# A written-out instruction order in place of a list scheduler: forward and backward of a strided convolution with group norm and GELU

## The chip, the cores and the metric

The kernel runs on one core of a Trainium2 chip. The metric is the device time of one execution in microseconds (us); smaller is better. A core has five engines that run side by side, each in its own program order: TensorE (PE: matmuls, with the weight loads shown as PEld), VectorE (DVE), ScalarE (ACT), GpSimdE (POOL) and SyncE (SP, which here only issues DMAs). SBUF holds the operands, PSUM (eight banks) the matmul sums. Engines wait for each other by semaphores.

## The reference

`x` is (2, 16000, 256), `w` (31, 256, 256), all in bfloat16. The forward part is a convolution over time with stride 2 and 31 taps, a normalisation of every channel over all 7985 output positions, scale and shift, and a tanh-GELU:

```python
    L = (T - K) // s + 1                     # s = 2, L = 7985
    h = sum over i of einsum('blc,cd->bld', x[:, i:i + s*L:s, :], w[i])
    mu, var = mean and variance of h over l
    h = (h - mu) / jnp.sqrt(var + 1e-5)
    h = h * gn_gamma + gn_beta
    return _gelu(h)
```

The outputs are this forward result and, for a given `grad_out`, the gradients with respect to `x` (out_1), `w` (out_2), `gn_gamma` and `gn_beta`. So there are three convolutions' worth of matmuls: forward, input gradient, weight gradient.

## The kernel before

**Stages.** F0 is the forward convolution of batch 0, F1 that of batch 1 with the GELU work of batch 0 beside it, G0 the input gradient of batch 0 with the GELU work of batch 1 beside it, G1 the input gradient of batch 1, and W the weight gradient in nine combinations n = 0 to 8. Each batch is cut into four chunks c = 0 to 3. The convolutions are split in three (leaves A, B, C, sums of operands made on DVE) so that fewer multiplications are needed; the price is the elementwise work on DVE and ACT that makes the sums and puts the results together.

**PE and PSUM.** The PSUM banks form a ring of four tiles of two banks. In G0 and G1 a tile goes through `g_seed` (earlier results are put in: line L836 on ACT, L1392 on ACT, L1396 on DVE), `g_leaf`, `g_three_b` and `g_three_ac` (the matmuls, L1329; after those of `g_three_b` a copy L1356 on ACT), and `g_evac` (the result to SBUF: `keep`, L836 on ACT, or an addition L1428 on DVE). After the last g_evac of a chunk pair a DMA of 1 MB stores a part of out_1 (`load`, L547, on SP's queue); the buffer it reads is written again by a later g_evac. In F0 and F1 the matmuls are L741, with copies L777 and sums L821, L825 and evacuation L856. In W they are L1564, with copies L1666 and sums L1674 into PSUM; L1630 and L1634 (`pair_x`), L1645 and L1650 (`pair_d`) and L1730, L1735 (`leaf_d`) make the operands on DVE.

**GELU work.** For each of eight units of a batch: two scalings and squares (L1101, L1103 on ACT), a combination (L1106 on DVE), two sigmoids (L1108, L1110 on ACT), a scaling (L1112 on DVE), five products (L1116 on DVE), then sums (L1127 on ACT, L1129 on DVE) and DMA transposes (`turn`, L552, on SP). `e_load` and `e_comp` bring a chunk's gradient from DRAM (tiles hd and dyd) and scale it (L1211 and L1213 on DVE, or L1218 and L1220 on ACT), add it (L1222) and spread it (L1231).

**Queues.** The large loads, stores and transposes are all issued by SP, one after the other; POOL's queue has the stores of the staged gradient (`dl`). Names in DRAM: hd the staged h, dyd and yd the staged gradient and result, dld the sums of the gradient, vl sums of weights, zt zeros.

**What sets the order.** Every operation is first recorded with `add` (engine, estimated time, the operations that must come before it by 32-byte cells of memory: `preds`). `emit` then issues the 3224 operations in the order that `order()` gives and pins it, so that every engine has exactly this order. In the kernel before, `order()` works out a due time for every operation, going back from PE's work, with shifts by kind (`lead`) and by kind and part (`fine`), and `listing` (a list scheduler with its own estimates of engines and DMAs) takes, at each step, the operation that is ready and due first.

Of the kernel before, what the change touches and what calls it, by code (L numbers as in the profile page):

```python
# [37 lines left out]

class Plan:
# [3 lines left out]
    def __init__(self, tc):  # L43
# [7 lines left out]
        self.look = 13  # L51
        self.pads = (3122.5, 3149.5, 2842.0)
        self.lead = {
            "F0 f_evac last": -17.5,
            "F0 f_mm f_leaf": -492.5,
            "F0 f_mm f_outer": -63.0,
            "F0 f_mm f_three_ac": 6.0,
            "F0 f_mm f_three_b": 10.5,
            "F0 f_mm pe_turn": -521.5,
            "F0 f_outer forward": -60.0,  # L60
            "F0 f_seed forward": -47.0,
            "F0 load put": 16.0,
            "F0 tt f_sums": -81.5,
            "F0 tt second": 39.5,
            "F0 tt third": 10.5,
            "F0 turn x_load": -31.0,
            "F0 ve f_seed": -184.0,
            "F0 ve_neg f_seed": 62.5,
            "F0 w_sum w2_part": 38.5,
            "F0 zero x_load": 202.0,  # L70
            "F1 f_evac last": -66.5,
            "F1 f_mm f_leaf": -359.5,
            "F1 f_mm f_outer": -0.5,
            "F1 f_mm f_three_ac": -9.0,
            "F1 f_mm f_three_b": -13.0,
            "F1 f_three_b forward": -29.0,
            "F1 keep f_evac": -8.5,
            "F1 load f_evac": -6.5,
            "F1 load gelu_unit": 7.5,
            "F1 load out0_store": 27.5,  # L80
            "F1 tiny elem_finalize": -18.0,
            "F1 tiny fwd_stats": 17.0,
            "F1 tt f_sums": -78.5,
            "F1 tt gelu_unit": -45.5,
            "F1 tt second": -72.0,
            "F1 tt third": -68.5,
            "F1 turn gelu_batch": 30.0,
            "F1 turn gelu_unit": -36.0,
            "F1 turn x_load": 44.5,
            "F1 ve f_seed": -25.5,  # L90
            "F1 w_sub f_again": 60.0,
            "G0 cp e_comp": -84.0,
            "G0 e_comp e_load": -1.0,
            "G0 g_evac last": -12.5,
            "G0 g_mm g_leaf": -8.5,
            "G0 g_mm g_three_b": -8.0,
            "G0 g_three_b input_grad": 0.5,
            "G0 gelu_batch conv_stem_kernel": -47.0,
            "G0 gelu_unit gelu_batch": -2.0,
            "G0 keep g_evac": -35.5,  # L100
            "G0 keep g_seed": -114.0,
            "G0 load dl_turn": 8.5,
            "G0 load e_load": 38.5,
            "G0 load g_evac": 17.0,
            "G0 load gelu_unit": 2.0,
            "G0 load load_w2": -0.5,
            "G0 spread e_comp": -1.0,
            "G0 tiny elem_finalize": -9.5,
            "G0 tiny fwd_stats": 6.5,
            "G0 tt first": -94.5,  # L110
            "G0 tt gelu_unit": -0.5,
            "G0 tt third": 5.5,
            "G0 turn dgb_store": 6.0,
            "G0 turn dl_turn": 5.0,
            "G0 turn gelu_batch": 7.0,
            "G0 w_sum load_w2": -5.5,
            "G0 zero e_comp": 10.0,
            "G1 cp e_comp": -166.0,
            "G1 e_comp e_load": 13.0,
            "G1 g_evac last": -8.0,  # L120
            "G1 g_mm g_leaf": -160.0,
            "G1 g_mm g_outer": -5.5,
            "G1 g_mm g_three_ac": -9.0,
            "G1 g_mm g_three_b": -33.0,
            "G1 g_three_b input_grad": -10.0,
            "G1 keep g_evac": 3.5,
            "G1 load dl_turn": 11.0,
            "G1 load e_load": -7.5,
            "G1 load g_evac": 9.0,
            "G1 plus g_seed": 1.5,  # L130
            "G1 spread e_comp": -6.0,
            "G1 spread g_seed": -69.0,
            "G1 tt first": -16.5,
            "G1 tt second": -15.0,
            "G1 tt third": -48.5,
            "G1 turn dl_turn": 3.5,
            "G1 w_sum w2_outer": 28.0,
            "G1 zero e_comp": -8.5,
            "W keep w_keep": -78.0,
            "W keep weight_grad": 6.0,  # L140
            "W leaf_d weight_grad": -3.5,
            "W load d_tile": -38.0,
            "W load out0_late": 111.0,
            "W load w_emit": 25.0,
            "W load weight_grad": 52.0,
            "W load x_raw": 1.5,
            "W pair_d weight_grad": -8.0,
            "W pair_x weight_grad": 0.5,
            "W turn out0_late": -42.5,
            "W ve weight_grad": -22.0,  # L150
            "W w_add weight_grad": 1.0,
            "W w_add x_tile": -2.0,
            "W w_both weight_grad": 10.0,
            "W w_emit w_done": -11.0,
            "W w_emit weight_grad": -353.5,
            "W w_mm w_leaf": -12.0,
            "W w_pairs weight_grad": -377.5,
        }
        self.spare = {k + " dl_turn": 3.0 for k in ("G0 turn", "G0 load", "G1 turn", "G1 load")}
        self.room, self.mixed = 2048.0, 2.2  # L160
        self.overlap = {"DVE": 0.084, "ACT": 0.1}
        self.fine = {
            "F0 f_evac last": {0: 23.0, 1: 16.0, 3: 6.5},
            "F0 f_mm f_outer": {0: 131.5, 2: -265.5},
            "F0 f_mm f_three_ac": {0: -57.0, 1: -59.0, 2: -100.5, 3: -14.5},
            "F0 f_mm f_three_b": {1: 8.5, 2: 3.0, 3: -307.0},
            "F0 f_outer forward": {0: 78.5, 3: -25.0},
            "F0 f_three_b forward": {0: 23.0, 3: -69.5},
            "F0 load put": {1: 187.0, 3: 31.5},
            "F0 tt f_sums": {0: -63.0, 2: 5.5},  # L170
            "F0 tt second": {0: 23.5, 1: -168.0, 2: -53.0},
            "F0 tt third": {1: -19.0, 2: -173.5, 3: -0.5},
            "F0 turn x_load": {0: 40.0, 1: 293.5, 2: 52.5, 3: 36.5},
            "F0 ve_neg f_seed": {0: 260.5, 3: 1.0},
            "F0 w_sub f_first": {0: 43.0},
            "F0 w_sum w2_part": {0: 20.0, 1: -74.5, 2: -56.0, 3: 42.0},
            "F0 zero x_load": {3: 7.0},
            "F1 f_evac last": {2: 13.5, 3: 12.0},
            "F1 f_mm f_outer": {3: -48.0},
            "F1 f_mm f_three_ac": {2: 20.0, 3: -4.0},  # L180
            "F1 f_mm f_three_b": {0: 3.0, 1: 48.0, 2: -3.0, 3: -35.0},
            "F1 f_three_b forward": {2: 29.5},
            "F1 gelu_unit gelu_batch": {0: -154.0, 2: -6.5, 3: -13.5, 4: 15.5, 5: -28.5, 6: 24.0, 7: -47.0},
            "F1 keep f_evac": {2: 6.5},
            "F1 load f_evac": {3: 3.5},
            "F1 load gelu_unit": {6: 11.0, 7: -15.5},
            "F1 load out0_store": {0: 7.0, 1: -8.0},
            "F1 tiny elem_finalize": {0: 6.0},
            "F1 tiny fwd_stats": {0: -42.0},
            "F1 tt f_sums": {0: 75.5, 1: -6.5, 2: 24.5},  # L190
            "F1 tt gelu_unit": {5: -38.0},
            "F1 tt second": {1: -25.5},
            "F1 turn gelu_batch": {0: -263.5, 1: -10.5, 3: 96.0},
            "F1 turn gelu_unit": {0: 0.5, 1: 30.5, 2: -17.5, 5: 40.5},
            "F1 turn x_load": {1: 40.5, 2: 9.5, 3: 27.5},
            "F1 ve f_seed": {1: 23.5, 2: 5.0},
            "F1 w_sub f_again": {3: -1.5},
            "G0 e_comp e_load": {0: -10.0, 1: -18.0, 2: -6.0, 3: -6.0},
            "G0 g_evac last": {1: 9.0, 2: 1.5},
            "G0 g_mm g_leaf": {0: -2.5, 2: -7.5},  # L200
            "G0 g_mm g_three_ac": {1: -1.0, 3: 19.0},
            "G0 g_mm g_three_b": {0: -3.0, 1: -5.0, 2: 1.5, 3: -22.0},
            "G0 g_three_b input_grad": {1: 5.0, 2: 14.0, 3: 6.0},
            "G0 gelu_batch conv_stem_kernel": {6: 40.0},
            "G0 gelu_unit gelu_batch": {0: -2.5, 1: -11.0, 3: 2.5, 4: -6.5, 5: -8.5, 6: -7.5},
            "G0 keep g_seed": {0: 122.0},
            "G0 load dl_turn": {0: -29.0, 1: 1.5, 2: -1.5},
            "G0 load e_load": {1: -41.0, 3: -1.0},
            "G0 load g_evac": {1: -16.0, 2: -6.0, 3: 10.5},
# [104 lines left out]
    def order(self):  # L314
# [3 lines left out]
        for i, o in enumerate(ops):  # L318
            for p in o["preds"]:
                succ[p].append(i)  # L320
# [1576 lines left out]
```

## Time and profile before

| what | value |
|---|---|
| time, median of 3 runs (lowest to highest) | 1166.46 us (1164.47 to 1167.01) |
| span of the profiled execution, first to last instruction | 1161.2 us |
| median less span (start and end around it) | 5.3 us |
| PE busy | 1128.5 us, 97% |
| DVE busy | 982.8 us, 85% |
| ACT busy | 554.0 us, 48% |
| POOL busy | 131.7 us, 11% |
| mean granted PE clock | 0.997 |
| moved by DMA | 243.57 MB, mean 210 GB/s |

The profile is one execution. Of the times, no row has the profiled execution's own total beside its span; the median of the runs stands in for it. A timeline row has the start, the busy time, the engine and the line, the operation with output and input, the count of equal instructions in a row, and in brackets the idle time before and what ended it. Successive rows of one engine can overlap by about 0.1 us. A matmul row's line is that of the helper, so tiles and times tell the stages apart: F0 and F1 are up to about 415 us, G0 and G1 to about 842 us, W to the end.

### The profile page before, as it was taken

The page shows a single profiled execution, that of the slowest core. Times are in us where ns is not written, and L with a number is a line of the kernel's source. Part 1 is how long each engine was busy: PE and PEld are TensorE (multiplying, and loading weights), DVE is VectorE, ACT ScalarE, POOL GpSimd, SP SyncE. Part 2 cuts the span into 40 slices and gives each one's busy share as a digit, 9 for nine tenths or more (in the row PEclk, how much of TensorE's full clock was granted, in tenths as well). Part 3 has the DMA queues.
Part 4 walks back from the last instruction along what each step waited for, and adds up shares of the span by engine and source line. Part 5 has one row for each costly group of instructions (what it writes and reads, how often), then busy time and mean ns, then how long its engine had stood idle before and what let it go on. Part 6 is the DMA issues. An engine that isn't in the chain of part 4 may idle for free.

```text
span 1161.2 us, 18913 instructions
## 1 busy us (share of the span) xinstructions
PE 1128.5 (97%) x7700; PEld 753.2 (65%) x7700; DVE 982.8 (85%) x892; ACT 554.0 (48%) x833; POOL 131.7 (11%) x221
## 2 busy tenths in 40 slices
PE   5999999999999999999899999999999999999998
PEld 3888899877777864444344444444488766656685
DVE  7996787699989988998786868768799998699986
ACT  1254454688786588788563545653422212211200
POOL 0000000000000011333232132241200000000000
PEclk9999999999999999999999999999999999999999
DMA  9476738869796699999996886686999726899673
GB/s 217 63 184 127 179 109 164 208 140 200 182 248 141 221 366 255 261 263 231 256 228 192 179 191 163 159 200 175 212 353 289 256 82 221 287 323 320 219 222 104
DMA packets 345807, 243.57 MB, mean 210 GB/s; under 512 B 233377, under 2 KB 316967, under 8 KB 341543
## 3 DMA queue, kind: packets, MB, share of 16 engines
q1 hardware_dynamic: 338615, 223.47, 73.5%
q0 software_dynamic: 7104, 18.89, 6.1%
q8 instruction: 60, 0.98, 0.4%
q14 instruction: 28, 0.23, 0.1%
HBM read 106.24 MB, written 80.25 MB: 161 GB/s over the span
## 4 chain that ended last, share of the span: by engine, by line
PE 80%; DVE 6%; DMA 6%; ACT 3%; SPq 3%; issue 2%; DVEq 0%; ACTq 0%
PE ps L741 33%; PE ps L1329 24%; PE ps L1564 22%; DMA arena<-dld 2%; SPq L547 2%; DMA out_dram<-arena 1%; DMA arena<-hd 1%; SPq L552 1%; DVE arena L1428 1%; ACT arena L836 1%; DMA arena<-dyd 1%; DVE arena L1116 1%; DVE arena L1282 1%; DVE arena L687 1%; DMA arena<-in_x_dram 1%
## 5 line engine op out<-in xcount | busy, mean ns | idle before, releaser
L1329 PE MATMUL ps<-arena 128*128 128x512 bf16 (+1 forms) x1920 | 414.0, 377 | 9.8 <-DVE arena L1428 3.2
L741 PE MATMUL ps<-arena 128*128 128x256 bf16 (+4 forms) x3460 | 406.8, 281 | 14.7 <-DMA arena<-in_x_dram 6.0
L741 PEld LDWEIGHTS <-arena 128*128 128x128 bf16 x3460 | 338.1, 99 | 83.2 <-DVE arena L683 6.4
L1329 PEld LDWEIGHTS <-arena 128*128 128x128 bf16 x1920 | 188.3, 98 | 233.6 <-issue 16.9
L1564 PE MATMUL ps<-arena 128*128 128x256 bf16 (+1 forms) x2320 | 309.2, 296 | 4.1 <-DMA arena<-dld 2.3
L1564 PEld LDWEIGHTS <-arena 128*128 128x128 bf16 x2320 | 226.8, 98 | 86.8 <-DMA arena<-dld 2.1
L836 ACT ACTIVATE arena<-ps 128x1024 f32<-128x1024 f32 (+1 forms) x111 | 113.1, 1022 | 248.9 <-PE ps L1564 86.1
L699 DVE TENSOR_TENSOR arena<-arena 128x2080 bf16<-128x2080 bf16 (+8 forms) x126 | 157.1, 1266 | 27.1 <-PE ps L741 26.4
L547 POOL DMA_DIRECT2D dld<-arena x144 | 104.6, 728 | 295.1 <-DMA arena<-arena 247.8
L1116 DVE TENSOR_TENSOR arena<-arena 128x2048 bf16<-128x2048 bf16 (+1 forms) x80 | 95.6, 1196 | 11.9 <-ACT arena L1110 5.8
L1282 DVE TENSOR_TENSOR arena<-arena 128x1032 bf16<-128x1032 bf16 (+1 forms) x120 | 84.5, 727 | 12.7 <-PE ps L1329 6.6
L1532 DVE TENSOR_TENSOR arena<-arena 128x4096 bf16<-128x4096 bf16 x38 | 86.1, 2285 | 7.9 <-DMA arena<-in_x_dram 5.5
L1396 DVE TENSOR_TENSOR ps<-ps,arena 128x2048 f32<-128x2048 f32 x24 | 55.1, 2298 | 22.3 <-PE ps L1329 21.4
L856 ACT ACTIVATE arena<-ps 128x512 bf16<-128x512 f32 (+1 forms) x64 | 37.0, 580 | 57.9 <-PE ps L741 53.7
L556 POOL MEMSET arena<- 128x128 bf16 (+11 forms) x40 | 8.6, 246 | 403.6 <-ACT ps L777 149.3
L1666 ACT COPY ps<-ps 128x256 f32<-128x256 f32 x54 | 19.3, 358 | 73.2 <-PE ps L1564 72.1
L1396 DVE TENSOR_TENSOR arena<-ps,arena 128x2048 f32<-128x2048 f32 x16 | 36.6, 2290 | 18.7 <-ACT arena L836 15.3
L1356 ACT COPY ps<-ps 128x512 f32<-128x512 f32 x48 | 27.5, 577 | 44.5 <-PE ps L1329 38.6
L1106 DVE SCALAR_TENSOR_TENSOR arena<-arena 128x2048 bf16<-128x2048 bf16 (+1 forms) x16 | 35.8, 2238 | 12.1 <-ACT arena L1103 12.1
L1428 DVE TENSOR_TENSOR arena<-ps,arena 128x1024 bf16<-128x1024 f32 x32 | 38.8, 1219 | 7.7 <-DMA out_dram<-arena 4.6
L1735 DVE TENSOR_TENSOR arena<-arena 128x4608 bf16<-128x4608 bf16 x16 | 40.5, 2552 | 5.7 <-PE ps L1564 5.6
L777 ACT ACTIVATE ps<-ps 128x256 f32<-128x256 f32 x75 | 27.8, 371 | 36.4 <-PE ps L741 35.1
(83 smaller groups left out, 780.4 us busy)
## 6 DMA issues: line engine op xcount, KB each, us to landing
arena<-in_x_dram SPq DMA_DIRECT2D x40, 1024.0 KB
dld<-arena POOLq DMA_DIRECT2D x144, 128.0 KB, 3.8
arena<-hd SPq DMA_DIRECT2D x32, 512.0 KB
out_dram<-arena SPq DMA_DIRECT2D x14, 1024.0 KB
arena<-dld SPq DMA_DIRECT2D x18, 640.0 KB
arena<-dld SPq DMA_DIRECT2D x18, 576.0 KB
vl<-arena SPq DMA_DIRECT2D x36, 256.0 KB
arena<-vl SPq DMA_DIRECT2D x9, 1024.0 KB
```

Of the source, the lines that this page charges most:

```text
L547: lambda: e.dma_start(out=out, in_=in_), dma=np_ * ns / 16e3 * 1.03, ns=ns, tp=SH[pk], slack=slack)
L699: lambda: nc.vector.tensor_tensor(out=o, in0=a, in1=b, op=ALU.add))
L741: yield nc.tensor.matmul(ps[:, dh, cs], lhsT=wt, rhs=mv, start=s0, stop=False, skip_group_check=True)
L836: lambda: nc.scalar.activation(out=out, in_=ps, func=ACT.Copy, scale=scale))
L1116: add("DVE", dve(nf), [o], [a, b_], lambda: V.tensor_tensor(out=o, in0=a, in1=b_, op=op))
L1282: lambda: nc.vector.tensor_tensor(out=o, in0=a, in1=b, op=ALU.subtract))
L1329: yield nc.tensor.matmul(ps[:, e, 0:wide], lhsT=lt, rhs=mv, start=s0, stop=False, skip_group_check=True)
L1396: lambda: nc.vector.tensor_tensor(out=o, in0=a, in1=b, op=ALU.add))
L1428: lambda: nc.vector.tensor_tensor(out=ho[:, :, k, :], in0=ps[:], in1=g, op=ALU.add))
L1532: add("DVE", dve(4096), [o], [a, b], lambda: nc.vector.tensor_tensor(out=o, in0=a, in1=b, op=ALU.add))
L1564: yield nc.tensor.matmul(ps[:, s, c0:c1], lhsT=lt, rhs=mv, start=s0, stop=False, skip_group_check=True)
L1735: add("DVE", dve(4608), [o], [u, v], lambda: nc.vector.tensor_tensor(out=o, in0=u, in1=v, op=ALU.subtract))
```

## The change

`order()` no longer computes anything. The order is a string of 3224 numbers, `SEQUENCE`; `order()` splits it, checks that it holds every operation once and that each comes after its `preds`, and returns it. The due times, the tables of shifts and `listing` are removed. The string stands for an order that was set by moving single instructions. The recorded operations, their operands and their count are the same. Every line after the edit is 237 lower (L836 is L599, L1428 is L1191, L1116 is L879, L1356 is L1119, L547 is L310, L552 is L315, L1218 and L1220 are L981 and L983, L1396 is L1159, L1231 is L994).

Of the operations, those that stand at another place on their engine are: PE 662 of 884 (an operation of PE is a group of matmuls), DVE 776 of 860, ACT 540 of 696, POOL 190 of 217, SP 520 of 567. The mean shift is 2.0 places on PE, 4.5 on DVE, 2.9 on ACT, 3.2 on POOL and 9.3 on SP.

```diff
+SEQUENCE = """
+6 12 5 4 13 3 7 15 9 1 11 22 14 8 2 16 17 31 37 41 32 34 38 40 33 35 23 42 39 36 44 52 25 43 53 50 46 45 47 49 26 48 51 55 24 56 61 54 66 27 67 29 62
...
+"""
...
-        self.fine = {
-            "F0 f_evac last": {0: 23.0, 1: 16.0, 3: 6.5},
...
     def order(self):
-        ops = self.ops
-        n = len(ops)
-        succ = [[] for _ in range(n)]
...
-            due[i] = end - full - self.lead.get(o["kind"], 0.0) - self.fine.get(o["kind"], {}).get(o["part"], 0.0)
-        self.listing(due, succ)
-        return sorted(range(n), key=lambda i: (self.start[i], i))
-
-    def listing(self, due, succ):
...
-                pick = min((i for i in w if ready[i] <= t + 1e-9), key=lambda i: (due[i], i))
...
-        self.start, self.ends = start, ends
+        seq = [int(i) for i in SEQUENCE.split()]
+        assert sorted(seq) == list(range(len(self.ops)))
+        seen = set()
+        for i in seq:
+            assert self.ops[i]["preds"] <= seen
+            seen.add(i)
+        return seq
```

Three places of the order follow.

The first is SP in G0, chunk 2, about 536 to 548 us of the profile before. The rows are DMA issues: a transpose of staged data (L552, L315 after), loads of dyd and hd for `e_load`, a store of the staged gradient dyd_2, the transpose of grad_out, the store of out_1 (out_dram<-arena) and a load of h for the GELU work (hd_3). Before:

```order
L552 DMA_TRANSPOSE arena<-arena 128x4x128 x4
L547 DMA arena<-dyd_0_72 128x2048
L547 DMA arena<-hd_0_64 128x2048
L547 DMA dyd_2_74<-arena 256x1x1024
L552 DMA_TRANSPOSE arena<-in_grad_out_dram 128x8x256
L547 DMA out_dram<-arena 128x4096
L547 DMA arena<-hd_3_67 128x2x1024
```

After:

```order
L315 DMA_TRANSPOSE arena<-arena 128x4x128 x4
L310 DMA dyd_2_74<-arena 256x1x1024
L310 DMA out_dram<-arena 128x4096
L310 DMA dld_8_88<-zt_117 2x256
L315 DMA_TRANSPOSE arena<-arena 128x4x128
L315 DMA_TRANSPOSE arena<-in_grad_out_dram 128x8x256
L310 DMA arena<-hd_3_67 128x2x1024
```

The store of out_1 stood behind the loads of dyd and hd and behind the transpose of grad_out; now it stands ahead of that transpose, and the two loads are elsewhere.

The second is ACT in G1, about 684 to 701 us, where `e_load` for chunk 1 of batch 1 comes up. The rows are copies out of PSUM (`keep`, L836, L599 after), the copies L1356 (L1119 after), and the scalings of hd (L1218, L981 after) and of dyd (L1220, L983 after). Before:

```order
L836 ACTIVATE arena<-ps 128x2x512
L1218 ACTIVATE arena<-arena,stats 128x1024 x2
L836 ACTIVATE arena<-ps 128x1024 x2
L1356 COPY ps<-ps 128x512 x2
L1220 ACTIVATE arena<-arena,stats 128x1024 x2
L836 ACTIVATE arena<-ps 128x2x512 x2
L1356 COPY ps<-ps 128x512
```

After:

```order
L599 ACTIVATE arena<-ps 128x1024
L1119 COPY ps<-ps 128x512
L599 ACTIVATE arena<-ps 128x1024
L1119 COPY ps<-ps 128x512
L981 ACTIVATE arena<-arena,stats 128x1024
L994 COPY arena<-arena 128x256
L599 ACTIVATE arena<-ps 128x2x512 x2
L1119 COPY ps<-ps 128x512
L599 ACTIVATE arena<-ps 128x2x512
L1155 COPY arena<-ps 128x2048
L599 ACTIVATE arena<-ps 128x2x512
L983 ACTIVATE arena<-arena,stats 128x1024
```

The scaling of dyd stood ahead of three `keep`s; now these stand ahead of it.

The third is DVE early in G0, about 438 to 452 us. The rows are g_evacs (L1428, L1191 after), GELU work (L1106, L1112, L1116; L869, L875, L879 after), sums for the next leaves (L1045 after) and the scaling of hd (L974 after, L1211 before). Before:

```order
L1428 TENSOR_TENSOR arena<-ps,arena 128x2x512
L1106 SCALAR_TENSOR_TENSOR arena<-arena 128x2048
L1112 TENSOR_SCALAR arena<-arena 128x2048
L1428 TENSOR_TENSOR arena<-ps,arena 128x2x512
L1116 TENSOR_TENSOR arena<-arena 128x2048
L1428 TENSOR_TENSOR arena<-ps,arena 128x2x512
L1116 TENSOR_TENSOR arena<-arena 128x2048
```

After:

```order
L869 SCALAR_TENSOR_TENSOR arena<-arena 128x2048
L1191 TENSOR_TENSOR arena<-ps,arena 128x2x512
L875 TENSOR_SCALAR arena<-arena 128x2048
L879 TENSOR_TENSOR arena<-arena 128x2048
L1045 TENSOR_TENSOR arena<-arena 128x1032
L1191 TENSOR_TENSOR arena<-ps,arena 128x2x512
L879 TENSOR_TENSOR arena<-arena 128x2048 x2
L974 TENSOR_SCALAR arena<-arena,stats 128x2048
L879 TENSOR_TENSOR arena<-arena 128x2048 x2
L1191 TENSOR_TENSOR arena<-ps,arena 128x2x512
```

Between the second and the third g_evac there was one product; now there are four products and a scaling.

More of the change, by code (lines that the diff above doesn't have):

```diff
@@ L50, in __init__ @@
         self.hold = -1
[L51 to L158, printed above, removed]
```

223 lines of the change are left out of this document (removed), and 100 rows, old and new, of the table SEQUENCE.

## The prediction

> **What bounds the kernel now.** I read the page first, then the list of waits of PE, then windows around each wait, then the timelines of the engines that PE waited for. The page's first rows (busy us, share of the span, instructions):
>
> ```profile
> span 1161.2 us, 18913 instructions
> PE 1128.5 (97%) x7700; PEld 753.2 (65%) x7700; DVE 982.8 (85%) x892; ACT 554.0 (48%) x833; POOL 131.7 (11%) x221
> ```
>
> PE is busy for 1128.5 of 1161.2 us. The change leaves its 7700 matmuls as they are, so it can only act on the other 32.7 us. PE's waits (us in total, times, longest) say what those are:
>
> ```profile
> PE ps L741 <- DMA arena<-in_x_dram: 6.0, 2, 4.6
> PE ps L741 <- DVE arena L683: 5.6, 1, 5.6
> PE ps L1329 <- DVE arena L1428: 3.2, 1, 3.2
> PE ps L1329 <- ACT ps L836: 3.1, 2, 1.8
> PE ps L1329 <- ACT arena L836: 2.4, 3, 1.9
> PE ps L1564 <- DMA arena<-dld: 2.3, 2, 1.6
> PE ps L741 <- DVE arena L699: 1.9, 1, 1.9
> PE ps L1329 <- ACT ps L1356: 0.7, 1, 0.7
> PE ps L1564 <- DVE arena L1532: 0.7, 1, 0.7
> PE ps L741 <- DVE ps L825: 0.6, 1, 0.6
> PE ps L1564 <- ACT arena L836: 0.6, 1, 0.6
> PE ps L741 <- ACT ps L777: 0.5, 1, 0.5
> PE ps L1564 <- ACT ps L1666: 0.4, 1, 0.4
> PE ps L1329 <- DVE ps L1396: 0.3, 1, 0.3
> ```
>
> They sum to 28.3. The first two rows and the seventh, 13.5 together, are the start of the program (first loads, first sums), before 29 us. The other 14.8 is spread over twelve places or so; the rest of the 32.7 is the store behind the last matmul. A wait can also cost a slower clock. Windows of 4 us around the two longest (columns: us; busy of PE, PEld, DVE, ACT, POOL with counts; granted clock; DMA; GB/s):
>
> ```profile
> 22.00:26.00 4.00, 2.94 (x16) 2.14 (x17) 4.00 (x4) 0.00 (x0) 0.00 (x0) 0.57 1.10 182
> 554.00:558.00 4.00, 0.85 (x5) 0.29 (x3) 1.88 (x2) 0.00 (x0) 0.00 (x0) 1.00 1.34 240
> 558.00:562.00 4.00, 4.00 (x12) 1.51 (x11) 3.90 (x4) 1.84 (x3) 2.89 (x4) 0.57 1.04 274
> 562.00:566.00 4.00, 4.00 (x21) 1.77 (x19) 2.59 (x5) 4.00 (x7) 1.44 (x3) 1.00 1.03 231
> ```
>
> After the wait that ends at 557.40 the clock is 0.57 for a window, and 12 matmuls run where the next window has 21. That costs (21−12)/21 × 4 = 1.7 us more, so that place is worth 3.2 + 1.7 = 4.9. [...]
>
> The start is left out of the sum: the ten vector operations between the first load and the first weight difference stand in the same order, without a gap. So is the end. The time of 1166.46 (median of the runs) is the span and 5.3 us around it, which I take as unchanged; what I save of the span I take off the median. About 0.2%, 2.3 us, is what a measurement of this kernel can tell from no change.
>
> **The change part by part.** Nothing is removed or added on any engine. What counts is what stands ahead of the instruction that PE waits for. A line after the edit is 237 lower (L836 is now L599).
>
> *The store in G0, chunk 2.* PE waits for a g_evac on DVE, and that for the 1 MB store of out_1:
>
> ```profile
> 557.40 2.84 PE L1329 MATMUL ps<-arena 128*128 128x512 bf16 x8 [3.15 <-DVE arena L1428]
> ```
> ```profile
> 539.57 7.70 SPq L552 DMA_TRANSPOSE arena<-in_grad_out_dram  x1
> 547.38 0.52 SPq L547 DMA_DIRECT2D out_dram<-arena  x1
> ```
> ```profile
> 540.49 1.22 DVE L1428 TENSOR_TENSOR arena<-ps,arena 128x1024 bf16<-128x1024 f32 x1
> ...
> 556.12 1.23 DVE L1428 TENSOR_TENSOR arena<-ps,arena 128x1024 bf16<-128x1024 f32 x1 [4.58 <-DMA out_dram<-arena]
> ```
>
> The store's data were ready at 540.49 + 1.22 = 541.7, but SP was in a transpose from 539.57 to 547.27, and the store was issued at 547.38. In the new order the store is ahead of that transpose and of the two loads (first piece of the order above). It can go out up to 547.38 − 541.7 = 5.7 us earlier; the wait to be covered is 3.15 for PE and 4.58 for DVE. Both ends: nothing if the store is held by something else, 4.9 if it goes. I take **4.9**. What is moved behind it, the transpose of grad_out, feeds GELU work that has no wait on PE in the list. Late next there is the ACT copy L836, below.
>
> *Two copies in G0 behind GELU work on ACT.* At 530 and 591 PE waits for a copy (L836, written to PSUM) which ACT starts only after a GELU instruction:
>
> ```profile
> 527.47 1.91 ACT L1108 ACTIVATE arena<-arena 128x2048 bf16<-128x2048 bf16 x1
> 529.28 1.01 ACT L836 ACTIVATE ps<-ps 128x1024 f32<-128x1024 f32 x1
> ```
> ```profile
> 588.60 2.20 ACT L1103 ACTIVATE arena<-arena,stats 128x928 bf16<-128x928 bf16 x2
> 590.70 1.00 ACT L836 ACTIVATE ps<-ps 128x1024 f32<-128x1024 f32 x1
> ```
>
> With 1.91 and 2.20 taken from in front of the copies, the waits of 3.1 go. At the second place the small copy L1356 of the next tile now has four GELU instructions of 1.1 (half of 2.20) ahead of it, so a part comes back: between 0 and the 1.8 of the row before; I take 0.8, the end nearest to the 0.7 that this copy costs in its own row of the list. Gain **2.3**.
>
> *ACT in G1.* PE waits 1.9 for a copy to SBUF behind a scaling that itself waits 6.92 for a load:
>
> ```profile
> 696.62 2.19 ACT L1220 ACTIVATE arena<-arena,stats 128x1024 bf16<-128x1024 bf16 x2 [6.92 <-DMA arena<-dyd]
> 698.71 1.92 ACT L836 ACTIVATE arena<-ps 128x1024 bf16<-128x1024 f32 x2
> ```
>
> The new order has these copies ahead of the scaling (second piece). The copies need only PE's result, so the 1.9 goes, and the 0.3 of L1396 just before it with it: **2.2**. The scaling is then later by two copies, 1.92; its result is for the next chunk, and no row of the waits names it. If that cover is gone, it costs 1.92.
>
> *Entry of W.* Three waits follow each other: 0.7 (L1356), 1.6 (load of dld), 0.4 (L1666), 2.7 together.
>
> ```profile
> 842.32 1.05 PE L1564 MATMUL ps<-arena 128*128 128x256 bf16 x8 [1.62 <-DMA arena<-dld]
> ```
> ```profile
> 838.83 2.30 DVE L1396 TENSOR_TENSOR ps<-ps,arena 128x2048 f32<-128x2048 f32 x1
> ```
>
> The dld loads now stand ahead of transposes on SP, and three blocks of PE work ahead of the weight-gradient blocks. PE would get there at 842.32 − 1.62 − 0.71 = 840.0, and the work moved forward needs L1396, which ends at 841.1. So 1.1 stays: **1.6**.
>
> *Short waits:* the rows L777, L825 and L836 of 0.5, 0.6 and 0.6 have more work between producer and PE in the new order: **1.7**. The rows of L1532 and the second of dld keep their neighbours: nothing.
>
> Gains: 4.9 + 2.3 + 2.2 + 1.6 + 1.7 = 12.7.
>
> *What it can cost.* In the first part of G0 PE has no wait now. There DVE makes eight g_evacs that free PSUM tiles, between GELU products (third piece of the order). In the new order the third one stands behind four products and one scaling:
>
> ```profile
> 445.27 1.23 DVE L1116 TENSOR_TENSOR arena<-arena 128x2048 bf16<-128x2048 bf16 x1 [1.00 <-ACT arena L1108]
> ...
> 456.59 0.70 DVE L1282 TENSOR_TENSOR arena<-arena 128x1032 bf16<-128x1032 bf16 x1
> 457.20 0.81 DVE L1211 TENSOR_SCALAR arena<-arena,stats 128x2048 bf16<-128x2048 bf16 x1
> ```
> ```profile
> 452.67 0.57 ACT L1356 COPY ps<-ps 128x512 f32<-128x512 f32 x1 [3.31 <-PE ps L1329]
> ```
> ```profile
> 439.74 18.51 PE L1329 MATMUL ps<-arena 128*128 128x512 bf16 x85
> ```
>
> From the first product at 445.27: product 1.2, sum 0.7, evac 1.2, four products 4.9, scaling 0.8, evac 1.2: it ends at 455.3, or 454.5 where each starts 0.1 before its forerunner ends. PE reuses the tile with four matmuls that ended by 452.67 (the copy started then); a matmul is 18.51/85 = 0.22, so they began at 451.8, and eight moved ahead of them make it 453.5. That leaves a wait between 1.0 and 1.8; I take **1.5**, since the sigmoids on ACT that the products need are packed closely too. It may hit none of the eight rows or all: 0 to 12. I take three, those that have four products ahead: **4.5**.
>
> New short waits elsewhere: 662 of 884 PE steps and most of DVE's and ACT's stand elsewhere, which no trace shows. The bound below is a gain of what is left of the short rows (about 1), above the mean of the list's rows of up to 0.7, 3.8 in 7, for fourteen places, 7.6. I take seven, **3.8**.
>
> Sum: −12.7 + 4.5 + 3.8 = −4.4, so 1166.5 − 4.4 = **1162.1**.
>
> **The rivals.**
>
> *A: the large store is not early.* SP issues DMAs in its own order, and if the store meets another full queue or a long transpose, the 4.9 stays: 1162.1 + 4.9 = 1167.0, no change. For it: the store's landing took from 547.38 to 556.1, so the transfers themselves are slow there (DMA share above 1 in the windows). Against: 5.7 us of lead on a wait of 3.15. Chance 0.15.
>
> *B: slower, through DVE in G0.* DVE is in order, and g_evacs queue behind products that wait for ACT's sigmoids. If all eight pay 1.5 it is 12 in place of 4.5: 1162.1 + 7.5 = 1169.6. With 12.7 gained and 3.8 lost in short waits, it becomes slower by more than 0.2% when this stretch costs over 11.2, that is from 7.5 of the eight rows on. For it: DVE is 85% busy, and four products have been put ahead of the evac. Against: a ring of four tiles, and PE has none of these waits now. Chance 0.17.
>
> *C: the entry of W waits for the last store of out_1.* Two pair_d differences (L1650) write where that store reads, and they now stand ahead of four w_both sums (L1674), which PE needs. If the store is late there as it was in G0, PE waits about that 3.15: 1162.1 + 3.2 = 1165.3, within the 0.2%. Against: a block of PE work has been put in between. Chance 0.11.
>
> **How the numbers follow.** The forecast's case has 0.57. Its own range goes from 1156.5, the gains whole with no evac wait and about 2.7 of short ones, to 1164.1, where faster ends. The whole range, 1156.5 to 1168.0, takes in A and C and leaves out B, 0.17, and some 0.03 below. Faster by over 0.2%: 0.57; within 0.2%: A and C, 0.26; slower: B, 0.17.
>
> **What would show it.** In the profile after: no PE wait for L1191 (was L1428) near 557 and no window with clock 0.57 there; the store's issue before the grad_out transpose; no wait for L599 near 530, 591 and 700; one wait of about 1 us at the entry of W, from L1159; the start's three rows as they were. New rows for L1191 between 420 and 510, of about 1.5 each, three of them. I am wrong if PE's busy time changes by more than 2 us (the clock), if the row of 3.2 is still there, or if the G0 rows are eight or none.

## The result and the profile after

The changed kernel takes 1150.56 us (median of 4 runs, 1149.26 to 1151.08); the kernel before, 1165.47 (4 runs, 1164.16 to 1167.01). The ratio is 0.9859, 95% interval 0.9835 to 0.9883: 1.4% faster, well over the 0.2% that can be told. That is 14.9 us, more than three times the 4.4 us of the forecast, and 1150.56 lies below its range. The profiled execution took 1151.08, with a span of 1149.3. So only 1.8 us lie around the span, not 5.3.

The first rows of the page of the changed kernel:

```profile
span 1149.3 us, 18868 instructions
PE 1123.6 (98%) x7645; PEld 753.3 (66%) x7700; DVE 984.2 (86%) x892; ACT 549.3 (48%) x833; POOL 126.6 (11%) x221
```

The trace lacks 55 matmul records, so PE's busy time can't be set beside that of before to the microsecond; DVE's is the same within 1.4. The waits of PE, all of them (us in total, times, longest):

```profile
PE ps L504 <- DMA arena<-in_x_dram: 6.5, 2, 4.8
PE ps L504 <- DVE arena L446: 4.9, 1, 4.9
PE ps L504 <- DVE arena L462: 2.1, 1, 2.1
PE ps L1092 <- DVE ps L1159: 1.3, 1, 1.3
PE ps L1092 <- ACT ps L1119: 1.3, 1, 1.3
PE ps L1327 <- DVE arena L1397: 1.1, 2, 0.8
PE ps L1092 <- ACT ps L599: 1.1, 1, 1.1
PE ps L1092 <- ACT arena L599: 0.5, 2, 0.2
```

The first three rows are the start, 13.5 as before. The rest adds up to 5.3, where the kernel before had 14.8. The row of L1191 (the 3.2 of L1428) is gone; the one at the entry of W is there, from L1159, as forecast. Around 553, where PE had stood for 3.15 (the window's columns as in the prediction):

```profile
552.00:556.00 4.00, 4.00 (x22) 1.91 (x20) 2.47 (x3) 3.97 (x3) 0.49 (x1) 1.00 1.00 263
```
```profile
544.23 0.34 SPq L310 DMA_DIRECT2D out_dram<-arena  x1
544.62 0.30 SPq L310 DMA_DIRECT2D dld<-zt  x1
544.97 2.02 SPq L315 DMA_TRANSPOSE arena<-arena  x1
547.04 3.86 SPq L315 DMA_TRANSPOSE arena<-in_grad_out_dram  x1
```

The store goes out first, PE is busy all the time, 22 matmuls run at full clock. The g_evac behind four products, which was priced at 1.5, in the timeline of DVE:

```profile
440.52 1.22 DVE L879 TENSOR_TENSOR arena<-arena 128x2048 bf16<-128x2048 bf16 x1
...
450.80 1.23 DVE L879 TENSOR_TENSOR arena<-arena 128x2048 bf16<-128x2048 bf16 x1 [0.93 <-DMA arena<-in_grad_out_dram]
451.94 1.22 DVE L1191 TENSOR_TENSOR arena<-ps,arena 128x1024 bf16<-128x1024 f32 x1
```

It ends at 453.2, before the 453.5 at which PE was worked out to need the tile, because the first product starts at 440.52 and not at 445.27; two waits on the way, 2.00 for ACT and 0.93 for a load, use up a part of the lead. No row of the waits names L1191. The prediction had called itself wrong if these rows were eight or none: they are none.

### The profile page after: what moved, and what is told of

It is laid out like the page before. It is cut to its first block, busy times and chain, and to the rows that moved or that the text cites. A ratio compares the mean times of both kernels' runs of the same rounds, so it can differ in the third digit from the quotient of the medians.

```text
span 1149.3 us, 18868 instructions
## 1 busy us (share of the span) xinstructions
PE 1123.6 (98%) x7645; PEld 753.3 (66%) x7700; DVE 984.2 (86%) x892; ACT 549.3 (48%) x833; POOL 126.6 (11%) x221
## 4 chain that ended last, share of the span: by engine, by line
PE 86%; DVE 8%; DMA 3%; issue 2%; ACT 1%; SPq 0%; DVEq 0%; ACTq 0%
PE ps L504 33%; PE ps L1092 33%; PE ps L1327 19%; DVE arena L1295 2%; DMA arena<-in_x_dram 2%; DVE arena L1397 1%; DVE ps L1437 1%; DVE arena L1413 1%; DMA dyd<-arena 1%; DVE arena L446 1%; DVE arena L462 0%; DMA arena<-dyd 0%; DVE arena L1493 0%; DVE arena L641 0%; DVE arena L1498 0%
## 5 line engine op out<-in xcount | busy, mean ns | idle before, releaser
L504 PE MATMUL ps<-arena 128*128 128x256 bf16 (+4 forms) x3460 | 407.5, 282 | 13.7 <-DMA arena<-in_x_dram 6.5
L1092 PE MATMUL ps<-arena 128*128 128x512 bf16 (+1 forms) x1880 | 408.7, 377 | 6.4 <-DVE ps L1159 1.3
L599 ACT ACTIVATE arena<-ps 128x1024 f32<-128x1024 f32 (+1 forms) x111 | 112.2, 1023 | 252.2 <-PE ps L1327 93.6
L310 POOL DMA_DIRECT2D dld<-arena x144 | 104.1, 725 | 287.5 <-DMA arena<-arena 276.3
L879 DVE TENSOR_TENSOR arena<-arena 128x2048 bf16<-128x2048 bf16 (+1 forms) x80 | 95.6, 1198 | 9.8 <-ACT arena L873 4.2
L1045 DVE TENSOR_TENSOR arena<-arena 128x1032 bf16<-128x1032 bf16 (+1 forms) x120 | 83.3, 726 | 7.3 <-PE ps L1092 4.7
L1159 DVE TENSOR_TENSOR ps<-ps,arena 128x2048 f32<-128x2048 f32 x24 | 55.2, 2298 | 22.4 <-PE ps L1092 17.1
L1191 DVE TENSOR_TENSOR arena<-ps,arena 128x1024 bf16<-128x1024 f32 x32 | 38.9, 1221 | 16.7 <-PE ps L1092 14.4
L1159 DVE TENSOR_TENSOR arena<-ps,arena 128x2048 f32<-128x2048 f32 x16 | 36.6, 2290 | 13.3 <-ACT arena L599 7.7
L574 ACT ACTIVATE arena<-ps 128x512 f32<-128x512 f32 x56 | 30.4, 600 | 33.7 <-PE ps L504 17.8
L869 DVE SCALAR_TENSOR_TENSOR arena<-arena 128x2048 bf16<-128x2048 bf16 (+1 forms) x16 | 35.8, 2241 | 10.3 <-ACT arena L864 8.7
L1413 DVE TENSOR_TENSOR arena<-arena 128x2048 bf16<-128x2048 bf16 x36 | 43.2, 1223 | 0.1
```

Of the source, the lines that this page charges most:

```text
L310: lambda: e.dma_start(out=out, in_=in_), dma=np_ * ns / 16e3 * 1.03, ns=ns, tp=SH[pk], slack=slack)
L504: yield nc.tensor.matmul(ps[:, dh, cs], lhsT=wt, rhs=mv, start=s0, stop=False, skip_group_check=True)
L599: lambda: nc.scalar.activation(out=out, in_=ps, func=ACT.Copy, scale=scale))
L879: add("DVE", dve(nf), [o], [a, b_], lambda: V.tensor_tensor(out=o, in0=a, in1=b_, op=op))
L1045: lambda: nc.vector.tensor_tensor(out=o, in0=a, in1=b, op=ALU.subtract))
L1092: yield nc.tensor.matmul(ps[:, e, 0:wide], lhsT=lt, rhs=mv, start=s0, stop=False, skip_group_check=True)
```

## The experiments

The theory after the result: the gain sits in G0, from an order in which the DMAs, the GELU work and the g_evacs of several engines were moved together; the price of the late g_evacs was worked out with DVE's new order and ACT's old one. The rival: a few single moves (the store, three copies) carry it. Each kernel has the changed kernel's code; only the numbers of the string differ. Ratios are to the kernel before on the same chip. Differences to the changed kernel set chips side by side; on them the median of the kernel before lies between 1163.9 and 1165.5.

### Is the profile of before a typical execution?

Run e1, the order before, written out as a string:

```diff
-SEQUENCE = the changed order
+SEQUENCE = the order that the kernel before works out
```

> The order of the kernel before, written out as the string; the same instructions in the same order on every engine. Theory (the format gives nothing, and the profile shown of before was a short execution): the time is that of before, ratio 1.000 within 0.2%, and a second profile of this order has a span of about 1164, some 3 us more than the 1161.2 shown, with the extra time in PE's waits (28.5 there, 31 to 32 here). Rival (the 5.3 us around the span belong to this kernel, 1.8 to the changed one): the span is again 1161 and the time 1166.

Measured: 1163.88 (12 runs), ratio 0.9995 (0.9975 to 1.0015). The profiled execution has a span of 1159.8 and 26.3 of waits, so the second half of the theory failed: this one was short too, 1161.55 in time. But its 12 runs go from 1160.4 to 1169.2, and each is its span and 1.8.

Run e5, the changed kernel once more, nothing edited:

> The changed kernel itself once more, many executions beside the kernel before on the same chip. Theory (what the new order gains beyond the profile's 11.9 is that before's executions vary and the changed kernel's do not): 1150.5 median, 12 to 14 below before, all executions within 3 us of each other where before's spread over 11, the granted clock 0.997 in each. Rival (its four executions were close by chance): a spread of 6 or more, median 1152 to 1154.

Measured: 1150.57 (1148.99 to 1151.81, 4 runs), ratio 0.9874 (0.9843 to 0.9905). In the five comparisons the kernel before ran 103 times: 1158.3 to 1172.1, median 1164.3, mean granted clock 0.991 to 0.998, median 0.995. The changed kernel's eight runs lie within 2.8 us of each other, at 0.997 to 0.999. The small spread and the distance are as the theory expected. The profile of before that the prediction used had 0.997, more than the median. So the two profiles are 11.9 apart and the medians 13.7; the other 1.8 is in executions of before that no profile showed.

### What kept the store late

Run e2, the changed kernel with the loads and the transpose in front of the store again (SP):

```diff
+load dyd (e_load, chunk 3)
+load hd (e_load, chunk 3)
 store dyd_2
+transpose grad_out
 store out_1
 zeros to dld, transpose of dl
-transpose grad_out
```

> The changed kernel with one thing undone: on SP, around the store of out_1 in G0, chunk 2, the two loads of e_load and the transpose of grad_out stand ahead of the store again. Theory (the place of the store gave the 4.9): PE waits 2 to 3.2 for L1191 near 556 and the clock halves once: 1.5 to 4.9 slower than the changed kernel, 1152 to 1155.5. Rival (the store was late only because the queue was full there in the order before, and has 7 us of cover now): no wait, 1150.6 within 0.5.

Measured: 1160.43, ratio 0.9966 (0.995 to 0.9982), 9.9 slower than the changed kernel. Its trace on DVE and PE, and the window behind:

```profile
562.35 1.22 DVE L1191 TENSOR_TENSOR arena<-ps,arena 128x1024 bf16<-128x1024 f32 x1 [10.66 <-DMA out_dram<-arena]
```
```profile
563.63 2.72 PE L1092 MATMUL ps<-arena 128*128 128x512 bf16 x6 [7.05 <-DVE arena L1191]
```
```profile
564.00:568.00 4.00, 4.00 (x11) 1.52 (x10) 3.93 (x4) 0.57 (x1) 0.88 (x3) 0.50 1.04 279
```

The wait is twice that of before, with half clock behind it: the place on SP decides, but more than the prediction's account explains. So the two things were put back one at a time. Run e13, the loads alone:

```diff
+load dyd (e_load, chunk 3)
+load hd (e_load, chunk 3)
 store dyd_2
 store out_1
```

> The changed kernel with the two loads of e_load for chunk 3 issued before the store of out_1, as in the order before; the store stays ahead of the transpose of grad_out. Theory (each of the two loads and the transpose in front of the store costs part of the 9.9 of putting both back): 2 to 5 slower than the changed kernel, 1152.5 to 1155.5. Rival A (the transpose is all of it): 1150.6 within 1. Rival B (the loads are all of it, by filling the queues): 1159 to 1161.

Measured: 1156.39, ratio 0.9936 (0.9913 to 0.9959), 5.8 slower than the changed kernel. Run e14, the transpose alone:

```diff
 store dyd_2
+transpose grad_out
 store out_1
 zeros to dld, transpose of dl
-transpose grad_out
```

> The changed kernel with the transpose of grad_out issued ahead of the store of out_1, the two loads where the changed kernel has them. Theory: 4 to 8 slower than the changed kernel, a wait of PE for L1191 of 2 to 5 near 556 and one half clock. Rival A (the transpose is all): 1159 to 1161. Rival B (the loads are all): 1150.6 within 1, no such wait, since the transpose took 3.9 in the changed kernel and the store has 7 of cover.

Measured: 1150.21, ratio 0.9881 (0.9857 to 0.9905): the changed kernel's time within 0.4. Rival B holds: with the loads put off, the transpose, which the prediction blamed, costs nothing. SP in its trace:

```profile
539.98 2.86 SPq L315 DMA_TRANSPOSE arena<-in_grad_out_dram  x1
542.94 0.53 SPq L310 DMA_DIRECT2D out_dram<-arena  x1
```

The loads cost 5.8. With them in front the transpose adds to it: both together cost 9.9, and in that run (e2) the transpose held SP for 6.18, not for 2.86; why it takes longer there isn't shown. What the loads do is seen on SP with them early (first fence), and on ACT there (second):

```profile
532.57 5.53 SPq L315 DMA_TRANSPOSE arena<-arena  x4
547.57 0.33 SPq L310 DMA_DIRECT2D arena<-dyd  x1
547.94 0.43 SPq L310 DMA_DIRECT2D arena<-hd  x1
548.47 0.58 SPq L310 DMA_DIRECT2D dyd<-arena  x1
549.15 0.55 SPq L310 DMA_DIRECT2D out_dram<-arena  x1
```
```profile
547.16 0.39 ACT L994 COPY arena<-arena 128x256 bf16<-128x256 bf16 x1
```

SP issues nothing from 538.1 to 547.57. The load of dyd writes a buffer that ACT's spread L994 still reads until 547.55, and the store behind it on the queue waits as well. In the order before, ACT did this spread 20 us earlier, so the load didn't have to wait there:

```profile
527.17 0.40 ACT L1231 COPY arena<-arena 128x256 bf16<-128x256 bf16 x1
```

The changed order has copies, scalings and sums of the GELU work ahead of this spread, and it must put off the loads with the spread. In these runs, the order of one engine fits only the orders of the others.

The other side, run e3: the kernel before with the store alone moved (SP):

```diff
 store dyd_2
+store out_1
 transpose grad_out
-store out_1
```

> The kernel before with one instruction moved: the store of out_1 in G0, chunk 2, ahead of the transpose of grad_out on SP. Theory: the wait of 3.2 for L1428 near 557 and the half clock behind it go, 4.9 faster than before, about 1161; window clock 1.00 there. Rival (the next wait behind it takes its place, ACT's L836 at 591 or the transpose that is now later): 2 or less.

Measured: 1163.02, ratio 0.9997 (0.9976 to 1.0018): the rival. The wait for L1191 is gone, and this is what came in its place, on ACT and PE. (The profiled execution is the longest of the twelve, 1169.11, so the size of this wait need not be typical.)

```profile
566.50 2.22 ACT L864 ACTIVATE arena<-arena,stats 128x928 bf16<-128x928 bf16 x2 [6.20 <-DMA yd<-arena]
...
572.80 1.00 ACT L599 ACTIVATE ps<-ps 128x1024 f32<-128x1024 f32 x1
```
```profile
573.85 2.72 PE L1092 MATMUL ps<-arena 128*128 128x512 bf16 x6 [3.80 <-ACT ps L599]
```

The GELU work waits for the store of yd, later on SP now; the copy that PE needs stands behind that work. Run e11 moves this copy and two like it forward as well (ACT):

```diff
+copy into PSUM (g_seed) of chunks 1, 2, 2
 GELU scalings and sigmoids
-copy into PSUM (g_seed) of chunks 1, 2, 2
```

> The kernel before with four instructions moved: the store of out_1 ahead of the transpose of grad_out, as in the run that moved it alone, and on ACT three copies L599 into PSUM (g_seed of chunks 1 and 2) ahead of the GELU instructions that stood in front of them. Theory (the store's gain was lost because the wait went to those copies, 3.8 of PE behind GELU work that waited 6.2 for the store of yd): the waits for L599 near 530, 570 and 592 go, 6 to 9 faster than before. Rival (the next in line is late by as much, DVE's GELU products or SP): 3 or less.

Measured: 1162.28, ratio 0.9982 (0.9968 to 0.9996): 2.5 faster than before in its own comparison, against 6 to 9 expected. The waits named are gone, but for 0.65 near 534. The next in line:

```profile
578.65 1.02 PE L1092 MATMUL ps<-arena 128*128 128x512 bf16 x4 [3.72 <-ACT arena L599]
```

Another copy, behind two sigmoids. The GELU work that feeds them was late once more, now behind one of the moved copies, which itself waited for a g_evac on DVE (the timeline of ACT):

```profile
564.70 1.01 ACT L599 ACTIVATE ps<-ps 128x1024 f32<-128x1024 f32 x1 [7.29 <-DVE arena L1191]
565.62 2.20 ACT L864 ACTIVATE arena<-arena,stats 128x928 bf16<-128x928 bf16 x2
```

Four single moves, priced in the prediction at about 7 in this stretch, give about 2.

### Why the late g_evacs cost nothing

Run e4, the kernel before with DVE's changed order between 430 and 512 us alone:

```diff
-DVE, 430 to 512 us: order before
+DVE, 430 to 512 us: changed order
```

> The kernel before with DVE's order of the changed kernel in the first part of G0 alone (77 operations that start between 430 and 512 us), ACT as before. The prediction priced a g_evac behind four GELU products at 1.5 of PE wait, three times. Theory (the price was right for ACT's order of before, and ACT's sigmoids stand earlier in the changed kernel): new waits of PE for L1191 of 1 to 2 us between 440 and 510, 3 to 5 slower than before, about 1169.5. Rival (PE needs the tile later than was worked out, so the ring covers it whatever ACT does): no new wait for L1191, time of before within 1 us.

Measured: 1182.09 (6 runs), ratio 1.0158 (1.0127 to 1.0188): 18 slower, more than either side expected. The profiled execution is the shortest of the six, 1174.92. It has 15.5 of waits for L1191, of which 4.5 end at 517, behind the edge of the stretch, and 2.5 at 575, where the order before has its 3.15. The longest, near 460:

```profile
456.63 0.81 DVE L974 TENSOR_SCALAR arena<-arena,stats 128x2048 bf16<-128x2048 bf16 x1 [5.29 <-DMA arena<-hd]
457.36 2.48 DVE L879 TENSOR_TENSOR arena<-arena 128x2048 bf16<-128x2048 bf16 x2
459.75 1.22 DVE L1191 TENSOR_TENSOR arena<-ps,arena 128x1024 bf16<-128x1024 f32 x1
```
```profile
461.02 3.27 PE L1092 MATMUL ps<-arena 128*128 128x512 bf16 x8 [7.07 <-DVE arena L1191]
```

The mechanism of the prediction's rival B is real, and dearer than priced: the scaling ahead of the g_evac waits 5.29 for a load that SP issues late in the order before (from 449.52 on, against 435.38 in the changed kernel). Without these 5.29, PE's 7.07 would be 1.8, an estimate from these rows. So with ACT's order of before the prediction's 1.5 was about right for the products, and the load comes on top. Run e12, all five engines changed in the same stretch:

```diff
-DVE alone, 430 to 512 us: changed order
+PE, DVE, ACT, POOL, SP, 430 to 512 us: changed order
```

> The kernel before with the changed order inside the stretch from 430 to 512 us on all five engines, where the earlier run had DVE's alone and was 18 slower with 15.5 of waits for L1191. Theory (what covers the late g_evacs in the changed kernel is that ACT's sigmoids and SP's loads of hd stand earlier there too): no wait for L1191 over 0.5 in the stretch, time of before within 3. Rival (PE's own order before the stretch or DMAs issued before it matter): waits of 4 or more for L1191 stay.

Measured: 1169.63, ratio 1.0036 (1.0017 to 1.0056), 4.9 slower than before and so above the "within 3". PE inside the stretch:

```profile
433.46 78.35 PE L1092 MATMUL ps<-arena 128*128 128x256 bf16 x368 [1.63 <-ACT ps L599]
```

Waits for L1191 inside the stretch are gone; what is left stands at its two edges (1.6 at 433, 2.7 at 521, both for L599). So the cover is the other engines' order. No run moved ACT alone or SP alone; the rows of e4 give 5.29 to SP's load at the one g_evac where they can be read.

### Where the gain lies

Runs e6, e7 and e8, by the stage in which operations were recorded, the rest as before:

```diff
-all operations: changed order
+only those of G0 and G1 / only those of W / only those of F0 and F1: changed order
```

> The changed order for the operations recorded in G0 and G1 (input gradient, GELU of batch 1), the order before for all others. Theory (by the two profiles the waits and the half clock between 415 and 835 us fall from 10.8 to 2.9): 8 to 10 faster than before, and most of before's spread gone. Rival (as with the store alone, a part of the order that is taken alone gives its gain back in new waits at its edges): 4 or less.

> The changed order for the operations recorded in W (weight gradient), the order before for all others. Theory (by the profiles the waits from 835 us on fall from 4.7 to 2.5): 2 to 3 faster than before. Rival: no change, 0 to 1, since the wait at the entry only moves to L1159.

> The changed order for the operations recorded in F0 and F1 (forward, GELU of batch 0), the order before for all others. Theory (only the waits of 0.5 and 0.6 to 1.3 near 193 and 416 go): about 1 faster than before, 0.5 to 2. Rival (the state of the GELU work and of the DMA queues at the entry of G0 is what makes before's G0 waits): 4 or more faster.

Measured: G0 and G1 1182.60, ratio 1.0144 (1.0111 to 1.0177); W 1168.07, 1.003 (1.0008 to 1.0053); F0 and F1 1178.55, 1.0107 (1.0079 to 1.0135). All three are slower, while the whole is 14 faster. In the first, PE waits 13.2 at 422 us for one sum (L584) on DVE, where G0's early work of the changed order meets the forward part of the order before. The second has a wait of 2.8 for L1159 at 845, the third waits of 5.2 and 4.8 at 396 and 428, with a mean granted clock of 0.991 in that execution. Stages overlap in time, and these kernels cut through the overlap; they say little about the stages. So the next ones, e9 and e10, cut in time:

```diff
-changed order throughout
+order before up to 419 us, then changed / up to 597 us, then changed
```

> Cut in time: the order before up to the last matmul group of the forward part (about 419 us), and from there the changed order for all that is left, on every engine. Theory (nearly all of the gain is in G0, G1 and W, and a cut in time, unlike the choice by recorded stages, leaves the neighbouring operations together): 9 to 13 faster than before, with waits as in the changed kernel from 450 us on. Rival (the changed order of G0 needs what the forward part did early on DVE, ACT and SP for it): 5 or more slower than before, with new waits right behind the cut.

> Cut in time at the middle of chunk 3 of G0 (about 597 us): the order before up to there, the changed order for the rest. Theory (by the two profiles the changed kernel is 5.8 ahead at this point and 11.7 at the end): 5 to 6 faster than before, and before's spread remains, since its DMA-bound waits lie ahead of the cut. Rival (the parts only work as a whole): no gain, or slower.

Measured: 1152.77, ratio 0.9893 (0.987 to 0.9917), 12 faster; and 1166.56, 1.0012 (0.9998 to 1.0027), no gain, with a wait of 2.5 for L1191 behind the cut. From the start of G0 the new order gives nearly all; from the middle of G0's last chunk it gives nothing. Runs e15, e16 and e17 take pieces in the middle, the rest as before:

```diff
-changed order throughout
+changed order from 419 to 615 us / 640 to 840 us / 419 to 690 us only
```

> The kernel before with the changed order, on all five engines, for the operations that start between 419 and 615 us, which is G0; outside as before. Theory (G0's order carries most of the gain): 6 to 9 faster than before, no wait over 2 between 440 and 600, granted clock 0.997. Rival (G0's order only holds together with what follows, as the loads that it puts off fall on G1): 3 or less.

> The kernel before with the changed order, on all five engines, for the operations that start between 640 and 840 us, which is G1 and the entry of W; outside as before. Theory (the profiles put 3 us here): 2 to 4 faster than before. Rival: nothing, within 1.

> The kernel before with the changed order, on all five engines, for the operations that start between 419 and 690 us: G0, its far edge and the first part of G1; outside as before. Theory (G0's order carries the gain and the 5.7 at its far edge was an artefact of the cut at 615): 8 to 11 faster than before, no wait over 2 between 440 and 690. Rival (what G0 puts off always comes back as a wait where the order before begins again): 4 or less, with a wait of 3 or more right behind 690.

Measured: 1162.05, ratio 0.9992 (0.9969 to 1.0015); 1176.38, 1.0103 (1.0073 to 1.0133); 1157.32, 0.9937 (0.9914 to 0.996). G0 alone loses most of its gain at the edge: one wait of 5.7 (mean granted clock of that execution 0.995), since behind 615 us the order before has the scaling of hd ahead of two g_evacs. DVE there:

```profile
625.47 0.81 DVE L974 TENSOR_SCALAR arena<-arena,stats 128x2048 bf16<-128x2048 bf16 x1 [2.97 <-DMA arena<-hd]
626.20 2.35 DVE L1191 TENSOR_TENSOR arena<-ps,arena 128x1024 bf16<-128x1024 f32 x2
```

With the edge 75 us later it keeps 8.1, with a wait of 2.6 for L599 at that edge. G1 alone ends in a wait of 6.7 for L1413 at 873. Last, run e18, the changed kernel with W as before:

```diff
 changed order up to 827 us
-changed order of W
+order before of W
```

> The changed kernel up to the entry of W (about 827 us), and from there the order before for all that is left. Theory (by the profiles W's waits fall from 4.7 to 2.5): 1 to 3 slower than the changed kernel, 1151.5 to 1154. Rival (the order before of W adds an edge as well): 5 or more slower, with a wait over 3 between 827 and 880.

Measured: 1159.33, ratio 0.9942 (0.9924 to 0.996), 8.8 slower than the changed kernel: the rival. DVE there:

```profile
859.09 1.23 DVE L1413 TENSOR_TENSOR arena<-arena 128x2048 bf16<-128x2048 bf16 x1 [4.01 <-DMA out_dram<-arena]
860.23 2.36 DVE L1437 TENSOR_TENSOR ps<-ps,arena 128x1024 f32<-128x1024 f32 x2
```

This is the mechanism of rival C, the differences that wait for the last store of out_1, and it costs PE 5.3. In the changed kernel that store is issued at 841.8, here at 848.8; in the kernel before at 851.1, but there PE was 10 us further back.

## Why the prediction was wrong

The direction was right. Of the 11.5 us between 1162.1 and 1150.6 the profiles account as follows.

**"The time is the span and 5.3 us around it"** was the first step to fail, by 3.5. Every run of either kernel whose span is on record is its span and 1.8; by that, the execution in the profile of before took about 1163.0, and I set it against a median of 1166.46. The longer executions hold what this profile did not show. A lower clock is a part of it (median 0.995, against 0.997 in the profile); their waits are in no profile of this order. One profile gave no spread, and I took an unexplained remainder for a constant.

**"What it can cost", 4.5 for the g_evacs**, failed by its whole size. I took DVE's place from the new order and the start of the products, 445.27, from ACT's old one; in the changed kernel they start 4.7 earlier, and the load for the scaling among them is issued some 12 earlier (435.38, against 446.97 or just behind it). With DVE's order alone (e4) the cost is there and larger; with all engines' (e12) the waits are not. I asked what stands ahead of an instruction, but not whether that, too, had moved.

**Seven new short waits, 3.8**, were 2.7 in the first profile (1.3 and 1.1 near 510, 0.3 at 900) and 2.1 in the second (0.2, 1.1, 0.3, and 0.5 at 877): 1.1 or 1.7 too much.

**The gains, 12.7**, were right in sum. Middle waits and the half clock were 14.8 + 1.7 before; 5.3 − 2.7 = 2.6 of old waits is left: 13.9, that is 1.2 more. The waits of the start and the end gave 0.5. The terms 3.5, 4.5, 1.1, 1.2 and 0.5 make 10.8 of the 11.5; the rest is within the spread of the runs. One thing is not in this sum: at the start PE worked for about 4.2 us at half clock in the profile after (0.51 from 24 to 28 us) and for about 2.6 before (0.57 from 22 to 26), which by these windows takes some 0.8 back, an estimate.

**The store.** In the profile after its wait and half clock are gone, as forecast, and putting its place back costs 9.9, twice the 4.9. But the reason given holds only in part. In the order before, moving the store ahead of the transpose does remove the wait for L1191 (e3), yet the time doesn't change by more than the noise; in the changed kernel the transpose alone in front of it costs nothing (e14), and the loads do (e13). The weak point was that the wait could move on: "late next there is the ACT copy L836" was written down, but priced as a gain of its own, as if the copy's lateness were there to be removed whatever came before it. In the one profile of e3 the copy's wait grew to 3.8. That the 4.9 came out right in the whole is in part luck.

**Rivals.** A and C did not occur in the changed kernel, nor did B; e3 is near to what A gives, by another way, and e4, e16 and e18 show B's and C's mechanisms in kernels that change one part. They were real mechanisms, switched off by moves elsewhere in the same string.

**Entry of W:** 1.1 forecast to stay, 1.3 measured, from L1159 as said.

What stays open: which of ACT's and SP's moves in early G0 are needed, and the cause of before's spread; no profile fell on one of its long executions of over 1168. The nearest is e3's, of 1169.11 and one instruction apart: beside the 3.8 it has a wait of 3.5 for a load of dld near 1022, and its mean granted clock is 0.994; at that place the profile of before has waits of 0.7.

## What to carry to other kernels

When an order changes on several engines at once, work out the start of every predecessor in the new order before pricing a queue, and expect that a part taken alone can give its gain back at the edge where it meets the old order. A wait removed is worth its length only if the next instruction in the chain is not late by the same cause: here single moves priced at 7 gave about 2. And set a profile against the time of that execution: a remainder that isn't start and end is a sign that the profile isn't the median.

## What the runs showed of the hardware

The spread of one program: the order before ran between 1158.3 and 1172.1 with a clock of 0.991 to 0.998, the changed one within 2.8 us, at 0.997 to 0.999. In the profile before, taken in windows of 2 us from 30 us to the last matmul, the clock is below 0.99 in two: 0.55 and 0.60, from 558 to 562, behind the wait of 3.15. Behind the wait of 1.91 it is 1.00 (700 to 704 us). In the profile after no such window is below 0.99; the longest wait there is 1.35.

Between 2.62 and 3.72 us, the length of a wait alone doesn't tell whether half rate follows. PE's rows of three kernels (e10, changed from 597 us on; e17, changed from 419 to 690 us; e12, changed from 430 to 512 us), each with the window behind it:

```profile
559.93 2.32 PE L1092 MATMUL ps<-arena 128*128 128x512 bf16 x10 [3.72 <-DVE arena L1191]
```
```profile
560.00:564.00 4.00, 4.00 (x19) 1.78 (x19) 3.90 (x4) 1.26 (x2) 2.54 (x4) 1.00 1.08 282
```
```profile
694.69 2.58 PE L1092 MATMUL ps<-arena 128*128 128x512 bf16 x11 [2.62 <-ACT arena L599]
```
```profile
695.00:699.00 4.00, 3.95 (x19) 1.76 (x19) 4.00 (x5) 3.21 (x6) 0.25 (x1) 1.00 0.32 66
```
```profile
520.95 2.26 PE L1092 MATMUL ps<-arena 128*128 128x256 bf16 x7 [2.70 <-ACT ps L599]
```
```profile
521.00:525.00 4.00, 4.00 (x12) 1.52 (x12) 3.78 (x6) 3.54 (x5) 1.33 (x5) 0.57 1.23 202
```

Waits of 3.72 and 2.62 were followed by full clock, one of 2.70 by half. Another wait of 3.72, the one of e11 that ends at 578.65, has half rate behind it:

```profile
579.00:583.00 4.00, 3.62 (x12) 1.22 (x10) 4.00 (x5) 1.49 (x3) 0.00 (x0) 0.58 1.05 294
```
